# Attention scores with K=64 on two row halves, two units in one go, between the matmuls of a bilinear feed-forward part

## The chip, the cores and the metric

One core of a Trainium2 chip runs the whole program. The metric is the device time of one execution in microseconds (us). A run is told with the mean clock that the throttle granted to TensorE, as a share of full speed. The median of the kernel before was taken first on three runs, and again beside each set of experiments on the same chip.

## The reference

Eight batches of attention, eight heads of 64 dimensions, 576 positions. Heads 0 to 3 see the last 32 positions (local); heads 4 to 7 see the earlier positions of the same residue modulo 32 (strided). The result, 4608 tokens by 512, goes through a bilinear feed-forward part without another input.

```python
scores = scale * np.matmul(q, k.transpose(0, 1, 3, 2))
mask_local = (rel >= 0) & (rel < stride)
mask_strided = (rel >= 0) & (pos[None, :] % stride == pos[:, None] % stride)
... softmax over the masked scores ...
x = np.ascontiguousarray(attn_out.transpose(0, 2, 1, 3)).reshape(B * S, H * D)
a = x @ w_a
b = x @ w_b
return (a * b @ w_out).astype(np.float32)
```

## The kernel before

The feed-forward part is cut into tiles of 512 tokens and these into 16 slots each: twelve slots `ffn_ab` (four matmuls with `wa_sb`, four with `wb_sb`) and four slots `ffn_y` (twelve matmuls with `wo_sb`). Attention for later batches is put between and into the slots. A unit is half of a head pair: `S` scores it (TensorE), takes the exponential (ScalarE) and masks (VectorE); `V` multiplies by the values and normalises. A position such as 33.5 means the middle of slot 34 (between its wa and wb matmuls), 34 the end of slot 34. The code is abridged.

```python
def S_p(b, u):
    ...
    qz = [tl[0, c // 2, "q"]] * 2 if b == 0 else [x[c // 2] for x in qz_buf[b % 2]]
    st = pst.tile([128, 2, 512], F32, tag="st", name="st")        # two PSUM banks
    for i in range(G):                       # G = 3 (local) or 4 (strided)
        k0 = (G * half + i) * (LW if c < 2 else GP)
        for j in range(2):                   # the two heads of the pair
            d = slice(64 * j, 64 * j + 64) if b == 0 else slice(0, 128)
            nc.tensor.matmul(st[:, j, i * n:(i + 1) * n], lhsT=kT[d, c % 2, k0:k0 + 128],
                             rhs=qz[j][d, c % 2, k0:k0 + n], ...)

def step_VT(b, u):                           # V from batch 2 on
    o = psum4["o"].tile([128, 2, 512], F32, tag="o", name="o")    # two other banks
    for i in range(G):
        for j in range(2):
            nc.tensor.matmul(o[:, j, i * n:(i + 1) * n], lhsT=vt, rhs=p[:M, j, i * n:(i + 1) * n], ...)
    nc.scalar.activation(r, sums, ACT.Ln)             # 1 / sum = exp(-ln(sum))
    nc.scalar.activation(r, r, ACT.Exp, scale=-1.0)
    for j in range(2):
        nc.vector.tensor_mul(dst, o[:64, j, :W], r[:, j])

def ffn_ab(t, f, mid, ab=None):
    ab = [psum4["mm"].tile([128, TTOK], F32, tag="mm", name="mm") for _ in range(2)]   # from three mm banks
    ab_mm(t, f, ab, range(KD), mid)           # wa x4, mid(), wb x4
    nc.scalar.copy(a_sb, ab[0])
    nc.vector.tensor_mul(pf[:, f, :], a_sb, ab[1])
```

In the kernel before, a score uses K=128: `qz` holds q with the other head's rows zeroed, so the rows of the head that is not meant add nothing. Transposed k and q come from VectorE (`step_D`), in slots that a table `gs` gives, and go into place by DMA. PSUM has eight banks: three `mm`, two `st`, two `o`, one `tp`.

The softmax here doesn't subtract the row's maximum and nothing guards it: scores larger than these inputs give would overflow.

## Time and profile before

| what | value |
|---|---|
| time, median of 3 runs | 344.63 us (342.58 to 345.07) |
| span of the profiled run | 340.5 us at clock 1.00 |
| one period of 16 slots | 35.45 us, of it 31.1 for 144 wide matmuls |

The prediction shows the page's busy shares, a period by stretch, and the score units.

### The profile page before, as it was taken

The page shows a single profiled execution, that of the slowest core. Times are in us where ns is not written, and L with a number is a line of the kernel's source. Part 1 is how long each engine was busy: PE and PEld are TensorE (multiplying, and loading weights), DVE is VectorE, ACT ScalarE, POOL GpSimd, SP SyncE. Part 2 cuts the span into 40 slices and gives each one's busy share as a digit, 9 for nine tenths or more (in the row PEclk, how much of TensorE's full clock was granted, in tenths as well). Part 3 has the DMA queues.
Part 4 walks back from the last instruction along what each step waited for, and adds up shares of the span by engine and source line. Part 5 has one row for each costly group of instructions (what it writes and reads, how often), then busy time and mean ns, then how long its engine had stood idle before and what let it go on. Part 6 is the DMA issues. An engine that isn't in the chain of part 4 may idle for free.

```text
span 340.5 us, 6847 instructions
## 1 busy us (share of the span) xinstructions
PE 330.9 (97%) x2478; PEld 173.3 (51%) x2520; DVE 204.4 (60%) x400; ACT 203.4 (60%) x331; POOL 140.5 (41%) x249
## 2 busy tenths in 40 slices
PE   8999999999998999999999999999999999999995
PEld 6654555455554555555555545555555444444444
DVE  5767557757875965876588756784766234303331
ACT  5763855477768755876577658775688533223311
POOL 8935539997385534752475346533000000000000
PEclk9999999999999999999999999999999999999999
DMA  9999999999999399959997989889220110020002
GB/s 153 151 203 189 202 178 162 181 145 95 132 187 176 53 112 182 104 97 92 172 103 128 82 166 99 146 65 148 71 59 2 62 64 0 0 92 33 1 31 94
DMA packets 102242, 37.56 MB, mean 110 GB/s; under 512 B 77632, under 2 KB 97728, under 8 KB 102208
## 3 DMA queue, kind: packets, MB, share of 16 engines
q0 software_dynamic: 87760, 19.58, 63.6%
q1 hardware_dynamic: 14448, 17.53, 16.4%
q8 instruction: 20, 0.33, 0.4%
q14 instruction: 14, 0.11, 0.1%
HBM read 39.71 MB, written 9.44 MB: 144 GB/s over the span
## 4 chain that ended last, share of the span: by engine, by line
PE 77%; DMA 14%; ACT 2%; DVE 2%; issue 2%; POOL 1%; SPq 1%; DVEq 0%; ACTq 0%
PE mm L520 43%; PE mm L548 25%; DMA wb_sb<-in_moe_w_b_dram 6%; DMA wo_sb<-in_moe_w_out_dram 4%; PE st L340 4%; PE o L438 3%; DMA qz11s<-tq 2%; PE misc L153 2%; DMA out_dram<-y_sb 1%; DMA qz01s<-tq 1%; SPq L302 1%; ACT a_sb L537 1%; ACT xr L447 1%; DVE pf L538 1%; PE tp L247 1%
## 5 line engine op out<-in xcount | busy, mean ns | idle before, releaser
L520 PE MATMUL mm<-xT,wa_sb 128*128 128x512 bf16 x407 | 108.7, 379 | 0.9
L520 PE MATMUL mm<-xT,wb_sb 128*128 128x512 bf16 x409 | 108.0, 379 | 1.0 <-DVE pf L538 0.2
L538 DVE TENSOR_TENSOR pf<-a_sb,mm 128x512 bf16<-128x512 f32 x106 | 72.0, 679 | 47.4 <-PE mm L520 26.5
L548 PE MATMUL mm<-wo_sb,pf 128*128 128x512 bf16 (+2 forms) x447 | 98.0, 368 | 0.7 <-DMA wo_sb<-in_moe_w_out_dram 0.2
L537 ACT COPY a_sb<-mm 128x512 f32<-128x512 f32 x106 | 62.1, 586 | 44.8 <-PE mm L520 42.0
L520 PEld LDWEIGHTS <-wb_sb 128*128 128x128 bf16 x432 | 41.4, 98 | 49.2 <-issue 2.5
L548 PEld LDWEIGHTS <-pf 128*128 128x128 bf16 x456 | 41.6, 98 | 42.7 <-issue 0.5
L520 PEld LDWEIGHTS <-wa_sb 128*128 128x128 bf16 x432 | 38.2, 98 | 34.9 <-issue 0.2
L554 ACT COPY y_sb<-mm 128x512 f32<-128x512 f32 (+2 forms) x35 | 20.0, 571 | 46.7 <-PE mm L548 37.8
L447 ACT ACTIVATE xr<-o 64x576 f32<-64x576 f32 x48 | 31.1, 647 | 25.0 <-PE o L438 24.8
L348 ACT ACTIVATE p<-st 128x576 bf16<-128x576 f32 (+1 forms) x64 | 41.6, 651 | 6.7 <-PE st L340 6.2
L454 DVE TENSOR_TENSOR xT<-o,xr 64x288 bf16<-64x288 f32 x48 | 21.6, 450 | 31.5 <-ACT xr L448 31.0
L448 ACT ACTIVATE xr<-xr 64x576 f32<-64x576 f32 x48 | 32.8, 682 | 1.5
L452 DVE TENSOR_TENSOR xT<-o,xr 64x288 bf16<-64x288 f32 x48 | 21.6, 450 | 18.2 <-ACT xr L448 17.9
L682 POOL CAST pace<-pf 1x1 f32<-1x1 bf16 x53 | 11.6, 219 | 43.0 <-DVE pf L538 42.6
L218 POOL DMA_DIRECT2D vs<-in_v_dram x24 | 19.6, 818 | 9.1 <-issue 9.1
L358 DVE TENSOR_TENSOR p<-p,mask_l 128x576 int16<-128x576 int16 x32 | 14.5, 452 | 13.2 <-ACT p L348 13.2
L194 POOL DMA_DIRECT2D ql<-in_q_dram x24 | 16.0, 667 | 6.1 <-DMA wo_sb<-in_moe_w_out_dram 3.7
L194 POOL DMA_DIRECT2D kl<-in_k_dram x24 | 16.0, 666 | 5.8 <-issue 3.9
L185 POOL DMA_DIRECT2D natk<-in_k_dram x24 | 14.6, 611 | 4.0 <-issue 3.4
L185 POOL DMA_DIRECT2D natq<-in_q_dram x24 | 14.6, 610 | 0.0
L288 DVE STREAM_TRANSPOSE tk<-natk 128x512 bf16<-128x512 bf16 x18 | 12.8, 708 | 1.8 <-DMA natk<-in_k_dram 1.5
(116 smaller groups left out, 306.3 us busy)
## 6 DMA issues: line engine op xcount, KB each, us to landing
out_dram<-y_sb SPq DMA_DIRECT2D x35, 256.0 KB, 2.4
vl<-in_v_dram POOLq DMA_DIRECT2D x7, 384.0 KB, 7.1
kl<-in_k_dram POOLq DMA_DIRECT2D x24, 72.0 KB, 3.0
ql<-in_q_dram POOLq DMA_DIRECT2D x24, 72.0 KB, 3.5
vs<-in_v_dram POOLq DMA_DIRECT2D x24, 72.0 KB, 3.5
wo_sb<-in_moe_w_out_dram POOLq DMA_DIRECT2D x4, 384.0 KB, 12.1
natk<-in_k_dram POOLq DMA_DIRECT2D x20, 72.0 KB, 3.3
natq<-in_q_dram POOLq DMA_DIRECT2D x20, 72.0 KB, 3.2
```

Source lines behind the costliest of these rows:

```text
L185: nc.gpsimd.dma_start(out=t[32 * h:32 * h + n], in_=bass.AP(tensor=src.tensor, offset=(b * H + HL + h) * S * D, ap=[[RS * D, n], [YS * RS ...
L194: nc.gpsimd.dma_start(out=t[32 * h:32 * h + 32], in_=src[b, h].rearrange("(i y) d -> y i d", y=32))
L348: nc.scalar.activation(p[:M, :, :W], st[:M, :, :W], ACT.Exp, scale=scale)
L447: nc.scalar.activation(r, sums, ACT.Ln)
L448: nc.scalar.activation(r, r, ACT.Exp, scale=-1.0)
L452: nc.vector.tensor_mul(dst[:, W * half:W * (half + 1)], o[:64, j, :W], r[:, j])
L454: nc.vector.tensor_mul(dst.rearrange("d (p r) -> d p r", r=RS)[:, :, G * half:G * (half + 1)], o[:64, j, :W].rearrange("d (g p) -> d p g", ...
L520: nc.tensor.matmul(ps_, lhsT=w[:, kk, 128 * f:128 * (f + 1)], rhs=xT[:, kk, TTOK * t:TTOK * (t + 1)], start=(kk == first), stop=(kk == last))
L537: nc.scalar.copy(a_sb, ab[0])
L538: nc.vector.tensor_mul(pf[:, f, :], a_sb, ab[1])
L548: nc.tensor.matmul(y, lhsT=pf[:, f, 128 * j:128 * (j + 1)], rhs=wo_sb[:, f, c0:c0 + n], start=(f == 0), stop=(f == FD - 1))
L554: (nc.scalar.copy if act else nc.vector.tensor_copy)(y_sb, y)
```

## The change

Its intent: with K=64 on the two row halves of the array the two heads of a pair are computed at the same time. Since a switch between K=64 and K=128 costs something on entry and on exit, two units are scored in one go (step `P`). The second unit's scores need two more banks and take the outputs' pair `o`; in return the outputs of every first half go to `st`. The loads change so that q needs no zeros, and the schedule changes because a `P` fills both pairs of banks.

```diff
+FIRST_P = 3
 # step_D: q and k go in 32-row pieces to where the row halves want them
+                if b >= FIRST_P:
+                    buf = kT_buf[b % 2][z][:, c] if nm == "k" else qz_buf[b % 2][0][z][:, c]
+                    ...
+                            nc.sync.dma_start(out=buf[p0:p0 + 32], in_=t[64 * c + 32 * j:64 * c + 32 * j + 32, e])
-    def rezero(b):      # four memsets on GpSimd, gone
+    def bank_pair(x):
+        pool = pst if x == "st" else psum4["o"]
+        return pool.tile([128, 2, 512], F32, tag=x, name=x)
-    def S_p(b, u):
+    def S_p(b, u, bank="st"):
+        halves = b == 0 or b >= FIRST_P
-        st = pst.tile([128, 2, 512], F32, tag="st", name="st")
+        st = bank_pair(bank)
-                d = slice(64 * j, 64 * j + 64) if b == 0 else slice(0, 128)
+                d = slice(64 * j, 64 * j + 64) if halves else slice(0, 128)
+    def step_P(b, u):
+        S_p(b, u)
+        S_p(b, u + 1, "o")
+        for x in (u, u + 1):
+            S_x(b, x)
+            S_m(b, x)
 # step_VT
-        o = psum4["o"].tile([128, 2, 512], F32, tag="o", name="o")
+        o = bank_pair("st" if b >= FIRST_P and half == 0 else "o")
-             3: {32: "S0", 32.5: "S1", 33.5: "V0", 34: "S2", 35: "V1", 35.5: "S3", 36.5: "V2", 37: "S4", 38.5: "V3", 39: "S5",
-                 40: "V4", 41: "S6", 42: "V5", 43: "S7", 44: "V6", 45.5: "V7"}}
-    LATER = {-2: "S0", -1: "S1", 0: "V0", 1: "S2", 2: "V1", 3: "S3", 4: "V2", 5: "S4", 6: "V3", 7: "S5", 8: "V4", 9: "S6",
-             10: "V5", 11: "S7", 12: "V6", 13.5: "V7"}
+             3: {32: "P0", 33.5: "V0", 34.5: "V1", 36: "P2", 37.5: "V2", 38.5: "V3", 40: "P4", 41.5: "V4", 42.5: "V5",
+                 43.5: "P6", 44.5: "V6", 45.5: "V7"}}
+    LATER = {-2.5: "P0", -1: "V0", 0.5: "V1", 2: "P2", 3.5: "V2", 4.5: "V3", 6: "P4", 7.5: "V4", 8.5: "V5", 10: "P6",
+             11.5: "V6", 12.5: "V7"}
```

More of the change, by code (lines that the diff above doesn't have):

```diff
@@ L294, in step_D @@
                 t = tl[b, z, nm]
+                if b >= FIRST_P:
+                    buf = kT_buf[b % 2][z][:, c] if nm == "k" else qz_buf[b % 2][0][z][:, c]
+                    if nm == "k":
+                        buf = buf[:, PAD:] if z == 0 else buf[:, :RS * GP]
+                    for j in range(2):
+                        for e in range(2):
+                            p0 = 64 * j + 32 * e
+                            nc.sync.dma_start(out=buf[p0:p0 + 32], in_=t[64 * c + 32 * j:64 * c + 32 * j + 32, e])
+                    continue
                 for e in range(2):
@@ L303, in step_D @@
                                           in_=t[r0:r0 + 32, e])
-    def rezero(b):
-        for j in range(2):
-            for t in qz_buf[b % 2][j]:
-                nc.gpsimd.memset(t[32:64] if j == 0 else t[64:96], 0.0)
     def step_Tk(b, c):
@@ L324 @@
     ps = {}
-    def S_p(b, u):
+    def bank_pair(x):
+        pool = pst if x == "st" else psum4["o"]
+        return pool.tile([128, 2, 512], F32, tag=x, name=x)
+    def S_p(b, u, bank="st"):
         c, half, M, n, G = unit(u)
         kT = kT_buf[b % 2][c // 2]
-        qz = [tl[0, c // 2, "q"]] * 2 if b == 0 else [x[c // 2] for x in qz_buf[b % 2]]
-        st = pst.tile([128, 2, 512], F32, tag="st", name="st")
+        halves = b == 0 or b >= FIRST_P
+        qz = [x[c // 2] for x in qz_buf[b % 2]]
+        if halves:
+            qz = [tl[0, c // 2, "q"] if b == 0 else qz[0]] * 2
+        st = bank_pair(bank)
         if b == 0 and c >= 2:
@@ L501 @@
                  27.5: "V4", 28: "S6", 28.5: "V5", 29: "S7", 29.5: "V6", 30.5: "V7"},
[2 rows of a table removed]
-    LATER = {-2: "S0", -1: "S1", 0: "V0", 1: "S2", 2: "V1", 3: "S3", 4: "V2", 5: "S4", 6: "V3", 7: "S5", 8: "V4", 9: "S6",
-             10: "V5", 11: "S7", 12: "V6", 13.5: "V7"}
-    FN = {"Tk": step_Tk, "Tq": step_Tq, "S": step_S, "V": step_V, "X": step_X}
[2 rows of a table added]
+    LATER = {-2.5: "P0", -1: "V0", 0.5: "V1", 2: "P2", 3.5: "V2", 4.5: "V3", 6: "P4", 7.5: "V4", 8.5: "V5", 10: "P6",
+             11.5: "V6", 12.5: "V7"}
+    FN = {"Tk": step_Tk, "Tq": step_Tq, "S": step_S, "P": step_P, "V": step_V, "X": step_X}
     def run(b, slot):
@@ L673 @@
             do(i, zero_qz, 0, nc.vector, (jz,))
-        do(17, rezero, 1)
         for i, t in ((0, vl_buf[0]), (0, vs_buf[0]), (18, vl_buf[1]), (19, vs_buf[1])):
```

## The prediction

> **What bounds the kernel now.** I read first the page's busy shares and its 40 slices.
>
> ```profile
> PE 330.9 (97%) x2478; PEld 173.3 (51%) x2520; DVE 204.4 (60%) x400; ACT 203.4 (60%) x331; POOL 140.5 (41%) x249
> PE   8999999999998999999999999999999999999995
> ```
>
> TensorE is busy in every slice, so the end moves only with the work and the gaps on TensorE. The other engines matter where they make it wait. Next, one period of the feed-forward part (a tile of 512 tokens, 16 slots: twelve with eight 512-wide matmuls, four with twelve), with busy time by stretch:
>
> ```profile
> 169.26:204.71 35.45, 35.11 (x253) 18.27 (x256) 24.79 (x46) 24.92 (x41) 17.97 (x35) 1.00 0.92 119
> 204.71:240.16 35.45, 35.18 (x253) 18.34 (x256) 24.80 (x46) 24.92 (x41) 16.69 (x33) 1.00 0.90 118
> ```
>
> The columns are length, then PE, PEld, DVE, ACT, POOL. A period holds 144 wide matmuls, which start 0.216 us apart: 31.1 us. The rest, 4.35 us, is attention: 56 score and 56 output matmuls, 24 of each 96 wide and 32 of each 72 wide. The timeline of TensorE shows a score unit between wide matmuls:
>
> ```profile
> 201.70 2.75 PE L548 MATMUL mm<-wo_sb,pf 128*128 128x512 bf16 x12
> 204.29 0.21 PE L340 MATMUL st<-qz00l,kT0l 128*128 128x96 bf16 x1
> 204.34 0.21 PE L340 MATMUL st<-qz01l,kT0l 128*128 128x96 bf16 x1
> ...
> 204.55 0.81 PE L520 MATMUL mm<-xT,wa_sb 128*128 128x512 bf16 x3
> ```
>
> Starts are what counts (durations overlap): six 96-wide matmuls take 204.29 to 204.55, 42 ns each and no loss at either end. The 72-wide ones start 32 ns apart. Batch 0 already scores with K=64 on the two row halves, so the new form can be read in the same trace:
>
> ```profile
> 14.50 0.41 PE L334 MATMUL st<-nmask,ident 72*128 72x288 bf16 x2
> 14.84 0.30 PE L340 MATMUL st<-tq,kT0s 64*128 64x72 bf16 x8
> 15.07 0.20 PE L394 MATMUL o<-vl,p 128*128 128x65 bf16 x1
> ```
>
> Eight K=64 matmuls start within 14.84 to 14.95 (0.30 less one duration of 0.20): four pairs, 33 ns a pair, so two heads for the time of one. But the two mask matmuls take 0.245 and should have let the first start at 14.745, and the last pair should have let the next start at 14.98. About 0.094 us is lost on entry and again on leaving.
>
> **What the Trainium skill says.** "TensorEngine Tiling (Array Packing)", Key Properties: changing the tiling mode drains TensorE. The trace agrees: 0.094 us each way. The same page, Restrictions and Gotchas: different row tiles must not write one PSUM bank at a time; the code gives the two halves of a pair one bank each, as batch 0 does. "PSUM — Partial Sum Buffer", Engine vs sequencer instructions: ScalarE and VectorE queues are strict FIFO. That decides this case: below, a copy whose input has long been ready stands behind two activations. "Perfetto Trace Analysis", Matmuls: independent groups should rotate through different banks so that evacuation overlaps matmuls; after the change the score and output banks are each other's spare, which is what makes the pairing possible, and new waits with it.
>
> **The change part by part.** Batches 3 to 7 (five) are changed.
>
> *Score matmuls.* A pair of local units now costs 12 x 42.3 ns = 0.508 us; after it 6 x 42.3 + 2 x 94 = 0.442. A strided pair: 16 x 32.4 = 0.518, after it 8 x 33 + 188 = 0.452. So 0.066 us a pair, four pairs a batch, five batches: -1.3 us. The ideal halving would be 5 us; the drains eat three quarters.
>
> *DMA.* K and q now go in 32-row pieces in another order: 32 issues a batch on the SP queue, where there were 24, with the same bytes. At about 0.6 us an issue the queue has room in 35 us. Zeroing by GpSimd (four memsets, 1.05 to 1.16 us) goes; nothing in the chain waited for it.
>
> *Waits that go.* I subtracted what each matmul should take from the distance to the next start. After 95 us the true gaps (not one missing record of 0.216) are: 0.06 and 0.24 near 98 and 102; 0.58 + 0.67 where batch 3's fifth score unit waits for the DMA of q (107.9 to 109.4), and 0.41 + 0.07 + 0.17 after it; 0.26 at 145.3, DMA again; 0.24 each at 181.0 and 216.3. Sum 2.9 us. Strided scores come later after the change (batch 3 three slots, about 6 us), so these DMA waits should vanish: -2.9 us.
>
> *Waits that come.* The new schedule puts most output steps V in the middle of a slot, between its a and b matmuls. Then Ln and Exp of that V stand on ScalarE ahead of the slot's own copy a_sb, and the multiplications ahead of its product pf. (P is the paired scores, S the single score unit of before; a and b are the two 4-matmul groups of a slot.) In the twelve-matmul slots this costs nothing, as their bank is asked for two slots later. The kernel before has such steps only in batches 2 and 3; this is one, all engines:
>
> ```profile
> 71.75 0.42 PE L438 MATMUL o<-p,vl 128*128 128x96 bf16 x6
> 72.00 1.03 PE L520 MATMUL mm<-xT,wb_sb 128*128 128x512 bf16 x4
> 72.20 0.65 ACT L447 ACTIVATE xr<-o 64x576 f32<-64x576 f32 x1 [0.85 <-PE o L438]
> 72.88 0.68 ACT L448 ACTIVATE xr<-xr 64x576 f32<-64x576 f32 x1
> 73.12 1.03 PE L520 MATMUL mm<-xT,wa_sb 128*128 128x512 bf16 x4
> 73.59 0.59 ACT L537 COPY a_sb<-mm 128x512 f32<-128x512 f32 x1
> 73.60 0.91 DVE L452 TENSOR_TENSOR xT<-o,xr 64x288 bf16<-64x288 f32 x2 [1.53 <-ACT xr L448]
> 74.22 0.59 PE L520 MATMUL mm<-xT,wb_sb 128*128 128x512 bf16 x2
> ```
>
> V ends at t = 72.00. The copy releases its bank at 74.22, t + 2.22; wa started at 73.12, is through at 73.98, and wb stands 0.24 us for that bank. A score unit (0.26) lay between; without it the wait is 2.22 - 2 x 0.863 = 0.49. VectorE's muls end at t + 2.52, pf (0.69) and the release at t + 3.27.
>
> I then took from the built programs, before and after, which earlier tile each of the three mm banks held. As a check it explains the two waits at 181.0 and 216.3: there a of the next slot gets the bank of the a just before, copied late after a V; in batch 7 it gets b's, and no wait stands there. For the changed kernel:
> - V1 of batches 4 to 7, alone in mid-slot: 0.49 each.
> - V2 and V3 in neighbouring slots: the second V fills 0.25 of the first wait, leaving 0.24. In batches 4 to 7 the a that follows then gets the bank of the a before it, ready only 2.22 after the second V, where its turn comes at 1.10: 1.12. Sum 1.36 each.
> - V4 and V5 there: 0.24, then 0.19 for pf and 0.07 for the copy: 0.50 each.
> - Batch 3 has three such neighbours: 0.50, 0.50 and 0.43.
> - V7 of batch 3 and the first pair of batch 4 stand at the same point of one slot. The pair's second half wants the output banks that V7 has just filled: free at t + 2.56, reached at t + 0.22. One wait of 2.3 us.
>
> Four batches x 2.35 + 1.43 + 2.3 = 13.1 us of new waits.
>
> Elsewhere the pair's second half finds the output banks free, but barely: a V in mid-slot frees them after 2.56 us, its pair comes 2.6 us later plus the entry and the first half (0.2).
>
> Sum: -1.3 - 2.9 + 13.1 = +8.9 us; 344.6 becomes about 353.5. I take 353, since some of my waits may overlap.
>
> **The rivals.**
> 1. The change does what it wants: the chain is TensorE's, each unit halves, and waits come out even. For it: TensorE has no slack, and the gaps before were small. Then -1.3 to -4 us, about 342. Against it: all waits of this kind in the trace fit the rule above, and the order of ScalarE's queue after the change is certain from the built program.
> 2. Waits come, but ScalarE (60% busy) and VectorE catch up and half of them are filled: about +2 us, 347. For it: a stall gives the others time, and the longest type (1.12) occurs in no place of the trace before that another wait doesn't cover.
> 3. A worse one: two exponentials in a row plus Ln and Exp make ScalarE late also at the pairs, or more DMA issues make the scores of batch 3 wait as before: another +2 to +4, 357.
>
> **Range and chances.** Repeats of the kernel before spread over 2.5 us. The bank pattern can't change, but each wait is uncertain by about a quarter: 3 us on the sum. Rival 2 pulls down further than rival 3 up. I take 346 to 357. Slower by 2% means over 351.5, which 353 clears narrowly: 0.64; same 0.33; faster 0.03.
>
> **What would show it.** Right: score pairs start 42 or 33 ns apart with about 0.09 us lost at either end; TensorE's gaps of about 0.24, 0.49 and 1.1 us ahead of wa or wb, ended by ACT a_sb, each 2.22 us after a mid-slot V; one of 2.3 us inside the first pair of batch 4 (near 127 us), ended by VectorE; no DMA wait near 108; periods of about 37 us where there were 35.45. Wrong: periods at or under 35.4; gaps that end with a DMA; the two matmuls of a pair starting one after the other, 30 to 40 ns apart, so that no halving shows.

## More of the kernel before

TensorE's and VectorE's timelines of the kernel before around 108 us; the columns are start, length, engine, line, operation, output and inputs, count, and in brackets the idle time before and what ended it:

```profile
107.27 1.03 PE L520 MATMUL mm<-xT,wb_sb 128*128 128x512 bf16 x4
108.72 0.19 PE L340 MATMUL st<-qz10s,kT1s 128*128 128x72 bf16 x1 [0.42 <-DMA qz10s<-tq]
...
109.17 0.78 DVE L283 STREAM_TRANSPOSE tk<-kl 128x576 bf16<-128x576 bf16 x1 [2.48 <-DMA qz10s<-tq]
```

TensorE waits for the DMA that brings q of batch 3, and a second time, for the other head's, 0.7 us later. VectorE stands idle for 2.48 us at the same time, in front of a transpose of batch 4's k. (The bracket names another transfer, but this transpose starts 0.28 us after the last load of batch 4's local k lands: here 108.89 and 109.17.)

## The result, and the profile after

The changed kernel took 353.12 us (median of 4 runs, 352.55 to 357.23) and gave the right values; the kernel before, on the same chip, 343.61 (342.09 to 345.07). The ratio is 1.030, with a 95% interval of 1.021 to 1.040. Ratios here are the mean time of one kernel's fast runs over that of the other's in the same rounds, so not quite the ratio of the medians that I quote. The slowest run, 357.23, had a clock of 0.989; the others had 0.998 or 0.999.

The page of the changed kernel, busy shares and the granted clock in 40 slices of the span:

```profile
span 350.9 us, 6935 instructions
PE 335.4 (96%) x2520; PEld 167.7 (48%) x2520; DVE 206.8 (59%) x400; ACT 201.6 (57%) x331; POOL 134.6 (38%) x245
PEclk9999999999999999999999999999999999999999
```

The span grew by 10.4 us, the clock did not fall, and the other engines did about the same work (VectorE 2.4 us more, ScalarE and GpSimd less): the time is lost between TensorE's instructions. A period by stretch, which answers to the lines shown of before:

```profile
169.26:206.74 37.48, 35.92 (x258) 17.09 (x257) 25.44 (x47) 24.50 (x40) 17.44 (x35) 1.00 0.87 112
```

A period takes 37.48 us, 2.03 more than before, and TensorE's busy time is at least 1.5 us short of it, where it was short by 0.3. Now the place where a period loses most, in the timeline of all engines:

```profile
147.77 0.42 PE L457 MATMUL o<-p,vl 128*128 128x96 bf16 x6
...
148.24 0.65 ACT L466 ACTIVATE xr<-o 64x576 f32<-64x576 f32 x1
148.27 1.02 PE L539 MATMUL mm<-xT,wb_sb 128*128 128x512 bf16 x4
...
148.92 0.68 ACT L467 ACTIVATE xr<-xr 64x576 f32<-64x576 f32 x1
...
149.63 0.59 ACT L556 COPY a_sb<-mm 128x512 f32<-128x512 f32 x1
...
150.27 1.02 PE L539 MATMUL mm<-xT,wa_sb 128*128 128x512 bf16 x4 [0.97 <-ACT a_sb L556]
```

V3 of batch 4 is issued in the middle of a slot, behind that slot's wa. It ends at 148.02 (six starts of 0.0425), and its logarithm and exponential stand on ScalarE ahead of the copy of wa's result, although wa was through when V3 began. The copy starts at 149.63 and frees its bank at about 150.24, 2.22 us after V3's end. The next wa takes that bank and starts at 150.27. Between true starts 1.14 us are lost (0.97 in the bracket, because there a modelled end of the matmul before is subtracted).

Two units in one go, in TensorE's timeline:

```profile
105.28 0.38 PE L539 MATMUL mm<-xT,wb_sb 128*128 128x512 bf16 x1
...
105.60 0.30 PE L351 MATMUL st<-qz10l,kT1l 64*128 64x96 bf16 x6
105.73 0.29 PE L351 MATMUL o<-qz10l,kT1l 64*128 64x96 bf16 x6
...
105.96 1.04 PE L539 MATMUL mm<-xT,wa_sb 128*128 128x512 bf16 x4
```

The last wide matmul starts at 105.28 and needs 0.216, so the next could start at 105.50; wa starts at 105.96. The pair costs 0.46 us where two single units cost 0.51. Each unit of the pair takes about half its former time (0.13 us from its first start to the next unit's), and about a tenth of a microsecond is lost at either end.

The first pair of batch 4, in the same slot as V7 of batch 3:

```profile
129.52 0.42 PE L457 MATMUL o<-p,vs 72*128 72x72 bf16 x8
...
129.88 0.30 PE L351 MATMUL st<-qz00l,kT0l 64*128 64x96 bf16 x6
...
131.38 0.91 DVE L473 TENSOR_TENSOR xT<-o,xr 64x288 bf16<-64x288 f32 x2 [1.20 <-ACT xr L467]
...
132.35 0.30 PE L351 MATMUL o<-qz00l,kT0l 64*128 64x96 bf16 x6 [2.17 <-DVE xT L473]
```

V7 has filled the `o` banks. Logarithm, exponential and two multiplications later they are free, and only then can the second half of the pair be written: 2.33 us.

One wait was not foretold. Around 108 us, all engines:

```profile
107.69 1.03 PE L539 MATMUL mm<-xT,wa_sb 128*128 128x512 bf16 x4
108.58 0.78 DVE L284 STREAM_TRANSPOSE tk<-kl 128x576 bf16<-128x576 bf16 x1 [2.94 <-DMA natk<-in_k_dram]
...
109.86 0.81 DVE L369 TENSOR_TENSOR p<-p,mask_l 128x576 int16<-128x576 int16 x2
...
110.36 0.34 PE L457 MATMUL st<-p,vl 128*128 128x96 bf16 x4 [1.64 <-DVE p L369]
```

VectorE stands 2.94 us in front of batch 4's transpose of k, whose load is late; the masks that V2 of batch 3 needs stand behind it. TensorE loses 1.80 us. It is the stand that was already there before the change, at 109.17, and cost nothing visible then.

### The profile page after: what moved, and what is told of

It reads as the page before. It is cut to its first block, busy times and chain, and to the rows that moved or that the text cites.

```text
span 350.9 us, 6935 instructions
## 1 busy us (share of the span) xinstructions
PE 335.4 (96%) x2520; PEld 167.7 (48%) x2520; DVE 206.8 (59%) x400; ACT 201.6 (57%) x331; POOL 134.6 (38%) x245
## 4 chain that ended last, share of the span: by engine, by line
PE 73%; ACT 11%; issue 4%; DMA 4%; POOL 4%; DVE 3%; DVEq 0%; POOLq 0%; ACTq 0%
PE mm L539 41%; PE mm L567 23%; ACT a_sb L556 4%; ACT xr L466 3%; ACT xr L467 3%; PE st L351 2%; DMA vl<-in_v_dram 2%; PE st L457 1%; DMA out_dram<-y_sb 1%; DVE pf L557 1%; PE o L413 1%; DMA kl<-in_k_dram 1%; POOL vs L219 1%; PE o L457 1%; PE ab L539 1%
## 5 line engine op out<-in xcount | busy, mean ns | idle before, releaser
L539 PE MATMUL mm<-xT,wa_sb 128*128 128x512 bf16 x424 | 110.3, 379 | 4.8 <-ACT a_sb L556 2.9
L539 PE MATMUL mm<-xT,wb_sb 128*128 128x512 bf16 x424 | 110.1, 379 | 1.1
L567 PE MATMUL mm<-wo_sb,pf 128*128 128x512 bf16 (+2 forms) x456 | 99.3, 368 | 0.0
L539 PEld LDWEIGHTS <-wa_sb 128*128 128x128 bf16 x432 | 39.8, 98 | 51.4 <-issue 8.7
L359 ACT ACTIVATE p<-st 128x576 bf16<-128x576 f32 (+1 forms) x44 | 28.6, 650 | 17.0 <-PE st L351 16.8
L700 POOL CAST pace<-pf 1x1 f32<-1x1 bf16 x53 | 10.2, 193 | 54.1 <-DVE pf L557 53.7
L466 ACT ACTIVATE xr<-st 64x576 f32<-64x576 f32 x20 | 12.9, 647 | 25.5 <-PE st L457 25.4
L466 ACT ACTIVATE xr<-o 64x576 f32<-64x576 f32 x28 | 18.1, 647 | 11.8 <-PE o L457 11.5
L471 DVE TENSOR_TENSOR xT<-st,xr 64x288 bf16<-64x288 f32 x20 | 9.0, 450 | 20.6 <-ACT xr L467 20.5
L473 DVE TENSOR_TENSOR xT<-o,xr 64x288 bf16<-64x288 f32 x28 | 12.6, 450 | 11.1 <-ACT xr L467 10.8
L369 DVE TENSOR_TENSOR p<-p,mask_l 128x576 int16<-128x576 int16 x32 | 14.3, 453 | 7.8 <-ACT p L359 7.4
L473 DVE TENSOR_TENSOR xT<-st,xr 64x288 bf16<-64x288 f32 x20 | 9.0, 450 | 15.0 <-ACT xr L467 14.9
L471 DVE TENSOR_TENSOR xT<-o,xr 64x288 bf16<-64x288 f32 x28 | 12.6, 450 | 7.3 <-ACT xr L467 7.2
```

What stands on the lines that cost most here:

```text
L359: nc.scalar.activation(p[:M, :, :W], st[:M, :, :W], ACT.Exp, scale=scale)
L471: nc.vector.tensor_mul(dst[:, W * half:W * (half + 1)], o[:64, j, :W], r[:, j])
L473: nc.vector.tensor_mul(dst.rearrange("d (p r) -> d p r", r=RS)[:, :, G * half:G * (half + 1)], o[:64, j, :W].rearrange("d (g p) -> d p g", ...
L539: nc.tensor.matmul(ps_, lhsT=w[:, kk, 128 * f:128 * (f + 1)], rhs=xT[:, kk, TTOK * t:TTOK * (t + 1)], start=(kk == first), stop=(kk == last))
L567: nc.tensor.matmul(y, lhsT=pf[:, f, 128 * j:128 * (j + 1)], rhs=wo_sb[:, f, c0:c0 + n], start=(f == 0), stop=(f == FD - 1))
```

## The experiments

Theory: the change loses because V in the middle of a slot puts its activations and multiplications ahead of the slot's own copy and product in first-in, first-out queues, and because the `P` of one batch meets the last V of the one before. The scores gain a little. Rivals: the drains of the mode switches cost more than the halving brings; the loads in 32-row pieces make TensorE wait; a V anywhere costs the same.

Eleven runs of nine kernels were made (e10 is e7 again, e11 is e8 again), all with right values. For spans I take the median over runs with a clock of at least 0.998, where there are any; for the kernel before these were 340.2, 340.7 and 340.35 in the three sets.

### e1: the slot's own copy and product first

TensorE's order is untouched. In a slot with a mid-slot V (other than the twelve-matmul slots) the part behind V's matmuls is emitted after the slot's copy and product, which changes the queues of ScalarE and VectorE. It also changes, in some slots, which of the three `mm` banks a tile gets; this shows in the built programs.

```diff
+        if defer:
+            pending.append((b, u, o))      # Ln, Exp and the multiplications of this V: later
+        else:
+            V_tail(b, u, o)
 ...
-                run(b, names)
+                run(b, names, pos % 1 == 0.5 and pos % 16 < 11)
 ... after the slot's copy and product:
+            while pending:
+                V_tail(*pending.pop(0))
```

> The changed kernel with TensorE's order untouched, but Ln, Exp and the multiplications of a mid-slot V queued on ScalarE and VectorE behind the slot's own copy a_sb and product pf. Queue-order theory: the 10.5 us of waits that end with a_sb or pf go (0.24, 0.57, 1.1 us ahead of wa or wb); what stays is the 2.3 us inside batch 4's first pair and the 1.8 us near 108; the output banks come free about 2.84 us after V, about when the second half of a pair asks (2.81), so under 0.1 us there. Time about 342.5, ratio to before 0.995. Rival (the pairing itself, its shared banks or its drains cost the time): no change, 351 to 354.

Measured: 345.74 us, median of 5; one run of 350.91 was slow. Ratio 1.0075 (1.0005 to 1.0144). The two runs of full clock had spans of 342.9 and 343.5. All waits for `a_sb` and `pf` behind a V are gone, and a period is 35.37 us, against 37.48. Around V3 of batch 4, where the changed kernel lost 1.14:

```profile
153.19 0.42 PE L457 MATMUL o<-p,vl 128*128 128x96 bf16 x6
153.41 0.59 ACT L568 COPY a_sb<-mm 128x512 f32<-128x512 f32 x1
153.44 1.03 PE L551 MATMUL mm<-xT,wb_sb 128*128 128x512 bf16 x4
...
154.02 0.65 ACT L475 ACTIVATE xr<-o 64x576 f32<-64x576 f32 x1
...
154.31 1.03 PE L551 MATMUL mm<-xT,wa_sb 128*128 128x512 bf16 x4
```

The copy comes first, the logarithm behind it, and wa follows wb without a gap. Where V2 to V5 of batches 4 to 7 made TensorE wait, the built program gives each tile the bank of the same earlier tile as in the changed kernel, so there (1.89 of the 2.46 us of waits in a period) it is queue order alone. At V1 (0.57) that isn't shown: in batch 4 wa starts at 146.31, while the product it waited for in the changed kernel still runs (146.18 to 146.83), because here it gets another bank.

The time is above the expected 342.5. Of 10.5 us the full-clock spans give back 8.1. The trace has the rest: VectorE's stand before the late k is longer (2.38 at 112.2, where it was 1.80), at 127.5 the second half of a pair waits 0.52 for `o`, and in each of four periods second halves wait some 0.33 in all. At 134.2 the 2.33 stays, where V7 meets the pair. The profiled run was the slow one: its clock was at half from 14.3 to 24.5 us, before any changed instruction, so I read only its waits.

### e2: every V at the end of a slot

```diff
-             3: {32: "P0", 33.5: "V0", 34.5: "V1", 36: "P2", 37.5: "V2", 38.5: "V3", 40: "P4", 41.5: "V4", 42.5: "V5",
-                 43.5: "P6", 44.5: "V6", 45.5: "V7"}}
+             3: {32: "P0", 33: "V0", 34: "V1", 36: "P2", 37: "V2", 38: "V3", 40: "P4", 41: "V4", 42: "V5",
+                 44: "P6", 45: "V6", 46: "V7"}}
+    LATER = {0: "P0", 1: "V0", 2: "V1", 4: "P2", 5: "V2", 6: "V3", 8: "P4", 9: "V4", 10: "V5", 12: "P6", 13: "V6", 14: "V7"}
```

> The changed kernel with every V at the end of a slot and pairs every four slots, so that P and V keep to the order of the kernel before. Queue-order theory: no wait on a_sb or pf, no collision of batch 3's last V with batch 4's first pair; left are 94 ns a side at 20 pairs and the wait near 108 for VectorE, which stands at the transposes of batch 4's k until that load has landed (1.8 to 3.5 us here, as TensorE gets there sooner). Time 341 to 343, ratio 0.99 to 1.0. Rival (pairing costs by itself): 350 or more.

Measured: 343.78 us (343.17 to 344.43, 4 runs), ratio 1.003 (0.997 to 1.009); median span 342.1. That is a little more than I had expected. The pairs and their loads are those of the changed kernel, and 9 us of span are back (342.1 against 351.3), by moving V to the ends of the slots and the pairs with it. TensorE still waits 0.17, 0.22 and 0.23 in a period, and once for VectorE:

```profile
109.89 0.29 PE L457 MATMUL st<-p,vl 128*128 128x96 bf16 x3 [2.17 <-DVE p L369]
```

So "a V anywhere costs the same" falls, and so does the rival that blames loads or drains for the 10 us.

### e3: batch 4's first pair half a slot later

```diff
-                steps.setdefault(pos, []).append((b, names.split()))
+                steps.setdefault(46 if (b, names) == (4, "P0") else pos, []).append((b, names.split()))
```

> The changed kernel with batch 4's first pair half a slot later, nothing else. The wait of 2.33 us inside that pair is for the output banks that batch 3's last V filled half a y slot (1.30 us) earlier now: 1.03 us should be left. In batch 4 the bank order also moves (the a after V3 gets the bank of a b), so its wait of 1.14 should become 0.20 and 0.08. Sum -2.2 us against the changed kernel: about 351, ratio 1.023. Rival (the wait is the drain or a DMA): unchanged at 2.3 us.

Measured: 353.02 us (350.10 to 354.33, 4 runs), ratio 1.029 (1.021 to 1.036). The times do not settle it: only one run had the full clock, with 350.10 us and a span of 348.4, 2.9 under the changed kernel's 351.3. The trace does. The wait inside the pair fell from 2.33 to 1.03, and batch 4's 1.14 to 0.20 + 0.08:

```profile
135.83 0.30 PE L351 MATMUL o<-qz00l,kT0l 64*128 64x96 bf16 x6 [0.87 <-DVE xT L473]
```

### e4: the changed schedule with K=128 scores

The schedule, the banks and the pairing of the changed kernel, with the zeroed q and the loads of before.

```diff
-                if b >= FIRST_P:
+                if b >= 99:                       # the loads of before
-        halves = b == 0 or b >= FIRST_P
+        halves = b == 0
+        do(17, rezero, 1)
```

> The changed kernel's schedule and banks, but K=128 scores against zero halves, with the DMAs and the memsets of before. Theory: every wait on a_sb, pf and the output banks stays as in the changed kernel, the drains go and each pair costs 0.51 in place of 0.44: +1.3 us, about 354.4, ratio 1.03 to 1.035. Rival (switching to row halves is what costs): back near the kernel before, 344 to 346.

Measured: 356.73 us (355.84 to 359.07, 4 runs; 354.4 had been expected), ratio 1.042 (1.035 to 1.049). The same waits stand in the same places (2.45 near 108.6, 2.31 inside the first pair of batch 4). A period takes 37.65 us against 37.48: four pairs, 0.17, so K=64 in pairs is worth 0.043 us a pair, or 0.9 us for all 20. In this schedule the loads in 32-row pieces make no wait of their own. The rest of the excess is clock: no run was above 0.995. The trace shows where:

```profile
111.24 0.43 PE L463 MATMUL st<-p,vl 128*128 128x96 bf16 x6 [2.28 <-DVE p L375]
111.51 1.69 PE L545 MATMUL mm<-xT,wb_sb 128*128 128x512 bf16 x4
112.99 1.91 PE L545 MATMUL mm<-xT,wa_sb 128*128 128x512 bf16 x4
```

After 2.3 us of idleness two groups of four wide matmuls take 1.69 and 1.91 us where such a group takes 1.03 otherwise.

### e5: batch 4's transposes of k and q three to four slots later

```diff
+                  4: (6, 7, 8, 9, 11, 12, 13, 14, 15, 17)}.get(b) or (      # slots of batch 4's transposes
                 3, 5, 7, 9, 11, 12, 13, 14, 15, 17)
```

> The changed kernel, with batch 4's transposes of k and q three to four slots later and nothing else. In the changed kernel's trace VectorE stands at about 106 to 108.6 before batch 4's transpose of k, whose load has not landed, and the mask of batch 3's second output pair stands behind it: TensorE waits 1.8 us at 108.3. My prediction had said that nothing would be left to wait there. Theory (the wait is VectorE's queue order, not batch 3's own operands): the wait goes, all else stays, -1.8 us: span 349, about 351.3 us. Rival (batch 3's own q or k is late, or another wait takes its place): no change, about 353.

Measured: 352.61 us (351.94 to 352.69, 4 runs), ratio 1.027 (1.022 to 1.032). In the trace the wait is gone. VectorE's masks for V2 and V3 come at 106.38, 3.5 us earlier:

```profile
106.38 1.00 DVE L369 TENSOR_TENSOR p<-p,mask_l 128x576 int16<-128x576 int16 x2 [0.16 <-ACT p L359]
```

The first half of batch 4's first pair comes at 127.81 where it came at 129.88. Of these 2.07 us, 0.24 were there at 102.4 already; the other 1.83 are the wait. But the time fell by only 0.5. All four runs had a clock of 0.994 or 0.995, and the profiled one shows why: behind the 2.33 us inside that pair TensorE runs at half clock. One-microsecond windows of it, whose last three columns are clock, DMA share and GB/s:

```profile
129.00:130.00 1.00, 0.00 (x0) 0.00 (x0) 0.67 (x2) 0.93 (x2) 0.00 (x0) 1.00 0.59 57
130.00:131.00 1.00, 0.71 (x7) 0.34 (x8) 0.69 (x2) 0.22 (x1) 0.00 (x0) 0.50 1.12 153
...
133.00:134.00 1.00, 1.00 (x5) 0.40 (x4) 0.00 (x0) 0.54 (x1) 0.00 (x0) 0.80 0.00 0
```

It is busy at half clock for a little over 3 us, which costs about 1.6 us. So the cause is confirmed in the trace, while the expected time (351.3) was missed.

### e6: K=64 one unit at a time in the schedule of before

```diff
-                d = slice(64 * j, 64 * j + 64) if b == 0 else slice(0, 128)
+                d = slice(64 * j, 64 * j + 64) if halves else slice(0, 128)
 # with the loads of the changed kernel; steps S0, S1, ... and all banks as before
```

> The kernel before, its schedule and banks, with one part of the change alone: from batch 3 on the score units use K=64 on the two row halves, one unit at a time. Theory: TensorE's rate of starts halves per unit (96 wide: 3 pairs instead of 6 matmuls, 0.254 to about 0.13; 72 wide: 0.259 to about 0.13), but each of the 40 units now pays entry and exit, 96 + 97 + 11 ns: +0.075 each, +3.0 us in all against the kernel before (ratio about 1.009). It shows why the two units of a pair must go in one go. Rival (drains cost nothing or the new loads matter more): -5 us, or more than +4 with DMA waits.

Measured: 347.87 us (345.75 to 349.14, 4 runs), ratio 1.013 (1.007 to 1.018); the one run of full clock had a span of 344.0, 3.3 over the kernel before's 340.7. In the trace a local unit costs 0.330 us (0.255 before) and a strided one 0.332 (0.258), and the second wide matmul behind each is about 0.01 late. Forty units make 3.4 us, a little over the expected 3.0. Waits for loads and banks after 90 us sum to 3.7 (half clock left out) where they summed to 2.95 before: near 110 TensorE waits 1.96 and 0.56 for transfers in 32-row pieces (the bracket names `kT1s`), where the kernel before waited 0.58 and 0.67 for its q. So this part of the change alone, without the pairing, is a loss. The halves do run side by side, but a unit of 0.26 us is too short to pay for two switches.

### e7 and e10: the change with its waits mended

e1's order, e5's transposes, and a schedule of batch 3 that ends early enough for batch 4's first pair:

```diff
+             3: {32: "P0", 33: "V0", 34: "V1", 35.5: "P2", 36.5: "V2", 37.5: "V3", 39: "P4", 40: "V4", 41: "V5",
+                 42.5: "P6", 43.5: "V6", 44.5: "V7"}}
```

> The change with three mends: in a slot with a mid-slot output step the slot's own copy and product go ahead of that step's activations and multiplications; batch 3's pairs and output steps half a slot to a slot earlier so that its last output step and batch 4's first pair no longer meet; batch 4's k and q transposes three to four slots later. Theory: gaps left about 0.11 a period and 0.5 in batch 3, so about 0.5 to 1.3 for all, scores -0.9, the before's 2.9 of gaps mostly gone: 1 to 3 us under the kernel before (ratio 0.991 to 0.997). Rival: the mends only move waits elsewhere, ratio 1.00 or above.

Measured: 340.31 us (339.52 to 344.45, 6 runs) against 342.98 for before, ratio 0.9945 (0.9886 to 1.0003). Two of its runs had a clock of 0.985 and 0.984.

> The kernel of e7 again, for the interval, since two of its six runs had a start at the lower clock: runs at a clock of 0.998 or above 2 to 3 us under the kernel before's, ratio 0.990 to 0.995, and 1.5 to 2 us under e9.

Measured: 340.24 us (340.06 to 340.38, 6 runs, all at 0.999 or 1.0) against 342.47, ratio 0.9934 (0.9905 to 0.9963); median span 338.55 against 340.35. This beats the kernel before by 0.7%, and the changed kernel by over 3%.

What is left: V now frees the `o` banks later, and the second halves of three pairs in a period wait about 0.11 us each. A period takes 35.37 us, 0.08 less than before: the pairs' gain of 0.17, and the 0.24 to 0.26 that each period of before lost, are mostly given back in these 0.33. Four such periods make 0.3 of the 1.8 us won; the rest lies before 130 us, where the waits of before near 108 are gone. No run has this schedule with K=128 scores; by e4's 0.043 us a pair, K=64 itself is worth 0.9 of the 1.8 (an estimate).

### e8 and e11: e2 with the late transposes

> The kernel of e2 (all output steps at slot ends, pairs every four slots) with batch 4's k and q transposes later. Theory: its wait of 2.33 us at 107.35 goes: -2.3 against e2 (ratio against the kernel before 0.996 where e2 had 1.003). Rival: another wait takes its place, ratio 1.00.

Measured: 340.39 us (340.16 to 340.59, 4 runs), ratio 0.991 (0.986 to 0.997); median span 338.7, 3.4 under e2's. In the trace the wait of 2.33 is gone. The two profiled runs differ by 2.6 (341.5 and 338.9), near the expected 2.3; what made e2's other runs up to 1.2 us longer than its profiled one I did not trace.

> The kernel of e8 again beside e10: about 0.6 us over e10 in runs of the full clock (its gaps 0.17 and 0.23 a period where e10 has 0.11), ratio against before 0.991 to 0.995.

Measured: 340.80 us (340.34 to 344.26, 6 runs), ratio 0.9966 (0.9927 to 1.0005); median span of the full-clock runs 339.1, 0.55 over e10's. One run at 0.989 widens its interval.

### e9: the kernel before with the late transposes

> The kernel before with batch 4's k and q transposes three to four slots later, nothing else: how much of what e7 and e8 win belongs to that move alone and not to the pairs. In the trace of before TensorE loses 0.58 + 0.67 near 108 (q's load) and 0.41 near 110; VectorE stands there too, for the same late loads. Theory: q's load still makes batch 3's strided scores wait, the rest goes, -0.4 to -1.2 us against before (ratio 0.997 to 0.999). Rival: VectorE's stand was all of it, -2 us or more (0.994), and then the pairs themselves win next to nothing in e7 and e8.

Measured: 343.28 us (341.73 to 346.19, 6 runs) against 342.47, ratio 1.003 (0.999 to 1.007); the three full-clock runs had a median span of 340.7 against 340.35. Nothing is won. TensorE comes to batch 3's strided scores a microsecond earlier and then waits as much longer for the same load of q (its last wide group before that starts at 106.28, in the kernel before at 107.27; the line is the first strided score):

```profile
108.63 0.19 PE L340 MATMUL st<-qz10s,kT1s 128*128 128x72 bf16 x1 [1.32 <-DMA qz11s<-tq]
```

In the kernel before, this matmul started at 108.72. In the profiled run TensorE also ran at half clock from 109.73 to 113.14, behind these waits. So the late transposes pay only where the strided scores come later, as in the paired schedules, and the gain of e7, e8 and e10 is not to be had from that move alone.

## Why the prediction was right

The prediction said 353.0 us (346 to 357) and slower with a chance of 0.64; it was 353.12 us and slower by 3.0%. The steps, each with what the trace of the changed kernel shows, in us:

| step | predicted | measured |
|---|---|---|
| score pairs, 20 | -1.3 | -0.9 |
| waits that go | -2.9 | -1.15: 2.95 gone, 1.80 new |
| V1 alone, batches 4 to 7 | 4 x 0.49 | 4 x 0.57 |
| V2 and V3, batches 4 to 7 | 4 x 1.36 | 3 x 1.38 and 0.52 |
| V4 and V5, batches 4 to 7 | 4 x 0.50 | 4 x 0.51 |
| batch 3, three neighbours | 1.43 | 1.47 |
| V7 against the first pair | 2.3 | 2.33 |
| sum | +8.9 | +10.7 |

The spans of the two profiled runs differ by 10.4.

- **The mechanism held.** The queue order of ScalarE sets the waits behind V2 to V5 of batches 4 to 7 (e1 removes them with TensorE's order, and the earlier tiles in their banks, unchanged; e2 by moving V), and the 2.22 us from V's end to the freed bank was read from one place of the kernel before and came back in every period. Rival 2, that half of the waits would be filled, is refuted: 1.14 and 2.33 stand whole. Rival 1 is refuted by the result, rival 3 in its cause: in the trace no pair but the one behind V7 waits for more than the switches, so neither the double exponentials nor the loads made them wait.
- **"These DMA waits should vanish"** was right to the letter and failed as a term. The strided scores did come late enough for q. But the same stretch holds VectorE's stand for batch 4's k; before, it lay beside TensorE's wait for q, and with that gone it became the wait itself, 1.80 us. e5 takes it away. I had listed TensorE's gaps with what ended each and had not asked what VectorE would do there next.
- **The size of the score term** was too large: the prediction's 0.066 us a pair measured 0.043 (e4). The cause is in the drain's account. Entry was 0.096 and exit 0.097, near the 0.094 read from batch 0, but the first two pairs of a burst start 53 ns apart (39 in a strided one) where later ones start 42 (32) apart, and the second wide matmul behind it is another 11 ns late, which the sum did not have.
- **V2 and V3 in batch 7** was misread from the table of banks: there a takes the bank of b, the wait is 0.20 + 0.08 behind the 0.24 and not 1.12. Too high by 0.84.
- **V1 alone** has the right size for another reason. The wait ends with VectorE's `pf` and not with the copy: V0's activations stand ahead of the copy that this `pf` needs, and V0's multiplications and a transpose ahead of the `pf` itself. V1's own copy frees its bank at about 141.8, before TensorE asks for it at 141.87, so the 0.49 of the prediction is hidden behind the 0.57. That is luck.
- The start of the sum was a median of 344.63; later medians of the same kernel were 342.0 to 343.6. A base 1.0 to 2.7 us high and a sum 1.8 too low met at 353. The exact hit is luck; the sign and most of the parts are not.

## What to carry to other kernels

When a step that needs other engines is moved between two halves of a fixed pattern, follow its followers into the first-in, first-out queues: here half a slot decided whether a copy whose input was ready stood behind 1.3 us of activations, and TensorE behind the copy. A mode switch of TensorE cost the same for a burst of one unit (e6) as of two (0.19 us in and out), so gather the work before switching, and count its banks. And when a wait is taken out of the sum, look at which other engine was standing in the same stretch; it may be the next to be waited for.

## What the Trainium skill lacked or had wrong

- "TensorEngine Tiling (Array Packing)", Key Properties: says that a change of tiling mode drains TensorE, but gives no size. Here it was 0.096 us on entry and 0.097 on exit, with the next wide matmul 0.011 late. With units of 0.26 us the drains outweigh the tiling: a single K=64 unit took 0.33 us where K=128 took 0.26 (e6).
- "TensorE: Matmul & The Clock Gate", Part 3: says that row tiles start about 4 ns apart. The two matmuls of a pair did here (3 to 4 ns). Pairs follow each other 32 ns (72 wide) or 42 ns (96 wide) apart, but the first two of a burst 39 and 53 ns. The page has no figure for this slower start of a burst.
- "TensorE: Matmul & The Clock Gate", Part 1, puts the fall to half clock after an idle window of about 3.4 us; Why this matters for your kernels advises against idle gaps over about 3 us. Here shorter gaps were enough: of the eight of 2.05 to 2.45 us in the profiled runs, five were followed by 3.41 us at 0.50 (e1 at 134 us, e4 twice, e5, e6; not the 2.33 of the changed kernel, nor the gaps of e1 at 112 and of e2 at 107), and so were two of 1.49 and 0.65 close together (e9). Each costs about 1.6 us. That the window runs freely, as the page says, fits the traces: in each of them all changes of clock within the run lie a whole number of 3.413 us apart. Cut into such windows, TensorE's busy share after 90 us (an estimate: each matmul from its start, for the distance to the next in an unbroken row) was 0.25 to 0.37 in the six windows before a fall, and 0.43, 0.47 and 0.48 in the lowest that were spared. So the window need not be idle, and where a gap lies in it decides. These figures are no sharp limit: two falls before 15 us (e1, e3) came after 0.46 and 0.47.
- "PSUM — Partial Sum Buffer", Engine vs sequencer instructions: strict FIFO is right, and the page leaves what it costs to the reader: 2.22 us from the last matmul of V to the release of a bank whose contents were ready before it (Ln 0.65, Exp 0.68, copy 0.59 and the steps between).
